# Attention and bilinear feed-forward on one core: the order of loads and of work in the opening list, the first weight block in halves, and eight weight columns in token halves

## The chip, the cores and the metric

The kernel runs on one core of a Trainium2 chip. The time is the device time of one execution in microseconds (us). The profile's span (first to last instruction) is about 1.8 us shorter than the time of the same run. Segments below are times in the span, and they come from profiled runs.

## The reference, cut to what matters

```python
# q, k, v: (8 batches, 8 heads, 576 tokens, 64);  bias_table: (32, 8)
scores = q @ k.T / 8 + bias_table[bucket(|i - j|)]      # per batch and head
attn   = softmax(scores) @ v
x      = attn.transpose(0, 2, 1, 3).reshape(4608, 512)
out    = ((x @ w_a) * (x @ w_b)) @ w_out                # 512 -> 1536 -> 512
```

The kernel works on pairs of heads: pair p is batch p // 4, heads 2(p % 4) and the next. The 576 tokens of a head are 512 in blocks of 128 and a tail of 64. The feed-forward part works in chunks of 512 tokens; a "weight column" is 128 of the 1536 columns of w_a or w_b.

## The kernel before

Pairs 8 to 31 run in a loop that is written as a pattern. What comes before, pairs 0 to 7 and the feed-forward inputs of chunk 0, is written as one list of tokens, in which each token is a few instructions. The order of the list is the order in which each engine gets its work.

```python
opening = """
    <k0 <q0 <k1 <q123h0 <k23 <tk <W0 <v0 <W1 <vtb <vta <tq <W2 <R0 <v1 <Wta <q123h1 <W3 <Wtb <R1
    <wa0 <k4 <wb0 <R2 <R3 <q4 <k5 <uq <q7 <q5 <wa1 <wb1 <k6 <uk <vt1b <k7 <vb1a <vb1b <vt1a <wa2 <q6
    <wb2 <wo TK0 PC0:A TQ0 PF1:D PX1:D PV1:A PU0:D CK0:A CQ00:D w1 S001 PX0:D CQ01:A S000 E001 E000
    # ... cut ...
    MT0 AV01 CX20:D M110 E111 N30 ET1 X30 M111 CQ31:A T2 ET2 S210 CX30:D E210 PF0:A LH FA0a N01 HA0a
    MT1 TK4 X01 T3 AV11 ET3 CX01:D S211 PU1:D FB0a FA1a E211 CK4:D HA1a N11 X11 G0a M210 S310 MT2
    # ... cut ...
    M73 M71 HA6f FB6f G6f AV50 N50 S62 ET6 MT6 E62 S61 FA7f HA7f M62 AV51 N51 TH S60 E61 M61 FB7f
    # ... cut ...
"""
for token in opening.split():
    step(token)
```

How to read a token:

| token | work | engine |
|---|---|---|
| `<q4 <k5 <v0 <vta <uq <wa0` | a load: queries, keys, values, tail values, tail queries of batch 1, a weight block | issued by GpSimd, in this order |
| `w1` | a filler matmul with zeros | TensorE |
| `TQ TK TZ`, `C...:A`, `C...:D` | transposes; the copy of their result, on ScalarE or VectorE | TensorE, then A or D |
| `S E M` | a block of scores, its exponential, its product with the band of bias values | TensorE, ScalarE, VectorE |
| `T ET MT`, `KS EK` | the same for the 64 tail tokens | the same three |
| `AV N X CX` | output of a pair, normalisation, its transposes, their copy | TensorE, VectorE, TensorE, A or D |
| `FA0a HA0a FB0a G0a` | weight column 0 of w_a for tokens 0 to 255, its eviction; the same of w_b; their product | TensorE, ScalarE, TensorE, VectorE |

`a` and `b` at the end of a weight column are the two token halves, `f` is all 512 tokens. The results of FA and FB go in turn to two PSUM banks, so a column has to wait until the one before the last is evicted.

```python
wrk   = ctx.enter_context(tc.tile_pool(name="wrk", bufs=2))
ps_ff = ctx.enter_context(tc.tile_pool(name="ps_ff", bufs=2, space=bass.MemoryType.PSUM))
XG = [wpool.tile([128, 5, 2, Dh], BF16, name=f"XG{i}") for i in range(2)]   # normalised output of pair p in XG[p % 2]

def ff_in(w, kind, c, df, lo, n):
    ps = ff_bank(f"{kind}{c}_{df}_{lo}")
    for mc in range(NMC):
        nc.tensor.matmul(out=ps[:, 0:n], lhsT=w[df // 4][:, mc, 128 * (df % 4):128 * (df % 4) + 128],
                         rhs=xn_sb[mc][:, 512 * c + lo:512 * c + lo + n],
                         start=(mc == 0), stop=(mc == NMC - 1))
    ff[kind, df, lo] = ps
```

The bias band (`<W`, `<R`, `<Wt`) is read from a table in memory that the kernel writes itself in its first microseconds, so the first band row in GpSimd's queue waits for that write.

The softmax here doesn't subtract the row's maximum and nothing guards it: scores larger than these inputs give would overflow.

## Time and profile before

| | before |
|---|---|
| time, median of 3 runs | 414.04 us (413.32 to 414.21) |
| span of the profiled run | 412.2 us |
| first weight column (FA0a) starts | 26.55 us |
| first score of pair 8, the end of the opening | 73.33 us |
| steady loop and end | 338.82 us |

The diff is in the opening alone, so the table cuts the span there. FA0a cuts the opening again. Ahead of it TensorE waits for ScalarE, VectorE and loads; after it TensorE is the bound. The page has one line on TensorE's granted clock, in tenths, in 40 slices of about 10.3 us:

```profile
PEclk9999999999999999999999999999999999999999
```

A 9 stands for 90% or more. The line says nothing about the time before the trace's first clock record, which here starts at 13.86 us; fillers of 0.61 us instead of 0.39 show half clock until then.

### The profile page before, as it was taken

The page shows a single profiled execution, that of the slowest core. Times are in us where ns is not written, and L with a number is a line of the kernel's source. Part 1 is how long each engine was busy: PE and PEld are TensorE (multiplying, and loading weights), DVE is VectorE, ACT ScalarE, POOL GpSimd, SP SyncE. Part 2 cuts the span into 40 slices and gives each one's busy share as a digit, 9 for nine tenths or more (in the row PEclk, how much of TensorE's full clock was granted, in tenths as well). Part 3 has the DMA queues.
Part 4 walks back from the last instruction along what each step waited for, and adds up shares of the span by engine and source line. Part 5 has one row for each costly group of instructions (what it writes and reads, how often), then busy time and mean ns, then how long its engine had stood idle before and what let it go on. Part 6 is the DMA issues. An engine that isn't in the chain of part 4 may idle for free.

```text
span 412.2 us, 8768 instructions
## 1 busy us (share of the span) xinstructions
PE 404.5 (98%) x3473; PEld 210.0 (51%) x3473; DVE 240.8 (58%) x568; ACT 251.3 (61%) x384; POOL 133.6 (32%) x191
## 2 busy tenths in 40 slices
PE   8999999999999999999999999999999999999996
PEld 3576656455555455455444555555545554444443
DVE  3898997366745665476656764667547652421320
ACT  4998992676748665677556765767486642322321
POOL 6967547788029300960079004300000000000000
PEclk9999999999999999999999999999999999999999
DMA  8999999999979914995299709960520012002004
GB/s 104 179 202 189 206 166 144 160 193 142 87 133 159 139 34 91 155 129 90 41 161 143 116 16 126 127 92 17 117 67 16 17 40 78 0 9 95 2 2 102
DMA packets 135786, 42.05 MB, mean 102 GB/s; under 512 B 113688, under 2 KB 130968, under 8 KB 135744
## 3 DMA queue, kind: packets, MB, share of 16 engines
q0 software_dynamic: 81712, 20.27, 56.3%
q1 hardware_dynamic: 48592, 11.87, 18.6%
q10 hardware_dynamic: 5440, 9.34, 7.2%
q8 instruction: 27, 0.44, 0.5%
q14 instruction: 15, 0.12, 0.1%
HBM read 39.18 MB, written 9.45 MB: 118 GB/s over the span
## 4 chain that ended last, share of the span: by engine, by line
PE 94%; DVE 2%; ACT 2%; DMA 1%; issue 1%; ACTq 0%; POOL 0%; POOLq 0%
PE pb L633 23%; PE pa L633 23%; PE po L670 22%; PE av L569 8%; PE qk L406 7%; PE av L559 2%; PE av L563 2%; PE qkh L446 1%; PE qkt L479 1%; DMA qn<-in_q_dram 1%; PE trb L321 1%; ACT ath L452 1%; PE trb L415 1%; PE trb L609 0%; DVE ath L461 0%
## 5 line engine op out<-in xcount | busy, mean ns | idle before, releaser
L430 ACT ACTIVATE at<-qk 128x1024 bf16<-128x1024 f32 x112 | 113.3, 1028 | 27.5 <-DMA out_dram<-ob 10.3
L643 DVE TENSOR_TENSOR g<-pb,ha 128x512 bf16<-128x512 f32 (+1 forms) x114 | 75.6, 664 | 75.0 <-PE pb L633 58.9
L633 PE MATMUL pb<-xn,wb 128*128 128x512 bf16 (+1 forms) x456 | 112.1, 368 | 0.2 <-DVE g L643 0.2
L633 PE MATMUL pa<-xn,wa 128*128 128x512 bf16 (+1 forms) x456 | 112.1, 368 | 0.0
L640 ACT ACTIVATE ha<-pa 128x512 f32<-128x512 f32 (+1 forms) x114 | 66.2, 581 | 67.7 <-PE pa L633 66.2
L670 PE MATMUL po<-wo,g 128*128 128x512 bf16 x420 | 98.2, 379 | 0.0
L435 DVE TENSOR_TENSOR at<-at,W 128x1024 bf16<-128x1024 bf16 x112 | 75.1, 686 | 22.2 <-ACT at L430 22.1
L633 PEld LDWEIGHTS <-wa 128*128 128x128 bf16 x456 | 41.2, 98 | 46.3 <-issue 6.6
L633 PEld LDWEIGHTS <-wb 128*128 128x128 bf16 x456 | 40.6, 97 | 43.6 <-issue 5.2
L670 PEld LDWEIGHTS <-g 128*128 128x128 bf16 x420 | 38.9, 98 | 44.9 <-issue 2.5
L675 ACT ACTIVATE ob<-po 128x512 f32<-128x512 f32 x34 | 20.4, 600 | 39.9 <-PE po L670 33.6
L569 PE MATMUL av<-vm,at 128*128 128x65 bf16 x896 | 41.2, 193 | 0.0
L569 PEld LDWEIGHTS <-at 128*128 128x128 bf16 x896 | 37.4, 97 | 6.3
L132 POOL DMA_DIRECT2D qn<-in_q_dram x48 | 36.4, 807 | 12.0 <-PE qk L406 6.9
L170 POOL DMA_DIRECT2D vt<-in_v_dram x12 | 7.4, 620 | 98.9 <-PE av L563 98.1
L580 DVE RECIPROCAL rc<-av 128x6 f32<-128x6 f32 (+1 forms) x64 | 11.9, 186 | 45.2 <-PE av L569 40.8
L141 POOL DMA_DIRECT2D kn<-in_k_dram x48 | 36.2, 794 | 1.4 <-issue 0.7
L559 PE MATMUL av<-vt,att 128*128 128x130 bf16 x152 | 33.6, 221 | 0.0
L406 PE MATMUL qk<-QB,KB 64*128 64x512 bf16 x192 | 29.1, 381 | 0.0
L582 DVE TENSOR_TENSOR XG<-av,rc 128x384 bf16<-128x384 f32 (+2 forms) x64 | 27.2, 425 | 2.2
L506 ACT ACTIVATE att<-qkt 128x640 bf16<-128x640 f32 x24 | 16.8, 701 | 13.0 <-PE qkt L480 13.0
L559 PEld LDWEIGHTS <-att 128*128 128x128 bf16 x152 | 15.0, 98 | 6.5
(104 smaller groups left out, 327.0 us busy)
## 6 DMA issues: line engine op xcount, KB each, us to landing
out_dram<-ob ACTq DMA_DIRECT2D x31, 256.0 KB, 3.1
vn<-in_v_dram POOLq DMA_DIRECT2D x16, 256.0 KB, 5.8
kn<-in_k_dram POOLq DMA_DIRECT2D x48, 64.0 KB, 5.0
qn<-in_q_dram POOLq DMA_DIRECT2D x48, 64.0 KB, 4.4
wa<-in_moe_w_a_dram POOLq DMA_DIRECT2D x3, 512.0 KB, 7.4
wb<-in_moe_w_b_dram POOLq DMA_DIRECT2D x3, 512.0 KB, 9.2
wo<-in_moe_w_out_dram POOLq DMA_DIRECT2D x1, 1536.0 KB, 15.6
xn<-XG SPq DMA_TRANSPOSE x52, 3.0
```

The lines of the kernel that those rows point to most:

```text
L132: nc.gpsimd.dma_start(out=by_tile(qn[b % 2])[:, h0 // 4, t, :, :], in_=q[b, h0:h1, 128 * t:128 * t + 128, :].transpose([1, 0, 2]))
L141: nc.gpsimd.dma_start(out=by_tile(kn[b % 2])[:, h0 // 4, t, :, :], in_=k[b, h0:h1, t:SM:NM, :].transpose([1, 0, 2]))
L406: nc.tensor.matmul(out=ps[:, hh, :], lhsT=kT[r, t, :], rhs=qT[r, :, :], start=True, stop=True)
L430: nc.scalar.activation(out=at[:, :, :], in_=ps[:, :, :], func=ACTF.Exp, scale=scale)
L435: nc.vector.tensor_tensor(out=at[:, :, :], in0=at[:, :, :], in1=w[:, :, S - 1 + t:S - 1 + t - SM:-1], op=MULT)
L559: nc.tensor.matmul(out=pav[:, slot, :, :], lhsT=weights_tail(p, jq), rhs=vt[i][:, :, hp, :], start=True, stop=True)
L569: nc.tensor.matmul(out=pav[:, slot, hh, :], lhsT=weights(p, t, hh, jq), rhs=vm[i][:, 2 * hp + hh, t, :], start=False, stop=True, skip_grou ...
L582: nc.vector.tensor_tensor(out=xg[:, jqs[0]:jqs[0] + m, :, :], in0=pav[:, 0:m, :, 0:Dh], in1=rc[:, 0:m, :].unsqueeze(3).to_broadcast([128, ...
L633: nc.tensor.matmul(out=ps[:, 0:n], lhsT=w[df // 4][:, mc, 128 * (df % 4):128 * (df % 4) + 128], rhs=xn_sb[mc][:, 512 * c + lo:512 * c + lo ...
L640: nc.scalar.activation(out=ha[:, 0:n], in_=ff["pa", df, lo][:, 0:n], func=ACTF.Copy)
L643: nc.vector.tensor_tensor(out=g_sb[df][:, lo:lo + n], in0=ff["pb", df, lo][:, 0:n], in1=ff["ha", df, lo][:, 0:n], op=MULT)
L670: nc.tensor.matmul(out=po[:, :], lhsT=g_sb[df][:, 128 * tt:128 * tt + 128], rhs=wo_sb[:, df, :], start=(df == 0), stop=(df == NDF - 1))
```

## The change

It has three parts. Loads: queries go first, and half of the values of batch 0 (four of its eight heads) and half of its tail values go ahead of the first band row, so that they no longer wait for the bias table. Weights: the first block of w_a and of w_b is stored and loaded in two halves, so that the first columns of both are there sooner. Work: eight weight columns instead of six are done in token halves, and the whole list after the loads is put in another order.

```diff
-    wa_sb = [wpool.tile([128, NMC, WC], BF16, name=f"wa{i}") for i in range(NW)]
+    wa_sb = [wpool.tile([128, 1 + (i == 0), NMC, WC // (1 + (i == 0))], BF16, name=f"wa{i}")
+             for i in range(NW)]
@@ (wb_sb the same) ... cut ... @@
-    def load_weights(src, dst, part):
+    def load_weights(src, dst, part, half):
+        c0 = WC * part + WC // 2 * half
+        n = WC // (1 + (part == 0))
         nc.gpsimd.dma_start(
-            out=dst[part][:, :, :],
-            in_=src[:, WC * part:WC * part + WC].rearrange("(m p) n -> p m n", p=128))
+            out=dst[part][:, half, :, :],
+            in_=src[:, c0:c0 + n].rearrange("(m p) n -> p m n", p=128))
@@ ... cut ... @@
-            parts = [(range(0, 6), 0, 256), (range(0, 6), 256, 256), (range(6, NDF), 0, 512)]
+            parts = [(range(0, 8), 0, 256), (range(0, 8), 256, 256), (range(8, NDF), 0, 512)]
@@ opening, ... cut ... @@
-        <k0 <q0 <k1 <q123h0 <k23 <tk <W0 <v0 <W1 <vtb <vta <tq <W2 <R0 <v1 <Wta <q123h1 <W3 <Wtb <R1
-        <wa0 <k4 <wb0 <R2 <R3 <q4 <k5 <uq <q7 <q5 <wa1 <wb1 <k6 <uk <vt1b <k7 <vb1a <vb1b <vt1a <wa2 <q6
-        <wb2 <wo TK0 PC0:A TQ0 PF1:D PX1:D PV1:A PU0:D CK0:A CQ00:D w1 S001 PX0:D CQ01:A S000 E001 E000
+        <q0 <k0 <q123h0 <tk <k23 <k1 <vta <v0 <W2 <W0 <tq <vtb <W1 <v1 <W3 <R0 <q123h1 <Wtb <Wta <R1 <k4
+        <q5 <wa0a <wb0a <k5 <uq <R2 <R3 <wa0b <wb0b <q4 <vt1b <wa1 <k7 <wb1 <k6 <q7 <vt1a <wb2 <uk <vb1b
+        <vb1a <wa2 <q6 <wo PU0:A w1 TQ0 PX1:A PC0:A PF0:D TK0 PC1:A CK0:D CQ00:A CQ01:A w1 S000 PV1:D
@@ ... cut ... @@
+        N01 M111 ET2 FA0a FB0a HA0a E210 T3 TZ0x CZ0x:A G0a FA1a HA1a MT2 AV11 ET3 M210 N11 S211 E211
+        FB1a G1a X01 TK5 CK5:D FA2a HA2a CX01:D S310 S311 E310 M211 FB2a FA3a G2a MT3 TQ4 E311 M311 TQ5
@@ ... cut ... @@
```

More of the change, by code (lines that the diff above doesn't have):

```diff
@@ L108 @@
     WC = DF // NW
-    wa_sb = [wpool.tile([128, NMC, WC], BF16, name=f"wa{i}") for i in range(NW)]
-    wb_sb = [wpool.tile([128, NMC, WC], BF16, name=f"wb{i}") for i in range(NW)]
+    wa_sb = [wpool.tile([128, 1 + (i == 0), NMC, WC // (1 + (i == 0))], BF16, name=f"wa{i}")
+             for i in range(NW)]
+    wb_sb = [wpool.tile([128, 1 + (i == 0), NMC, WC // (1 + (i == 0))], BF16, name=f"wb{i}")
+             for i in range(NW)]
     wo_sb = wpool.tile([128, NDF, DM], BF16, name="wo")
@@ L297, in load @@
         else:
-            load_weights(*((moe_w_a, wa_sb) if name[1] == "a" else (moe_w_b, wb_sb)), int(name[2]))
+            load_weights(*((moe_w_a, wa_sb) if name[1] == "a" else (moe_w_b, wb_sb)), int(name[2]), int(name[-1] == "b"))
     st = [dict() for _ in range(NP)]
@@ L628, in ff_bank, with block @@
         return ps_ff.tile([128, 512], FP32, tag="ffn", name=name)
+    def block(w, df, mc):
+        half, d = divmod(df % 4, 2) if df < 4 else (0, df % 4)
+        return w[df // 4][:, half, mc, 128 * d:128 * d + 128]
     def ff_in(w, kind, c, df, lo, n):
@@ L632, in ff_in @@
         for mc in range(NMC):
-            nc.tensor.matmul(out=ps[:, 0:n], lhsT=w[df // 4][:, mc, 128 * (df % 4):128 * (df % 4) + 128],
+            nc.tensor.matmul(out=ps[:, 0:n], lhsT=block(w, df, mc),
                              rhs=xn_sb[mc][:, 512 * c + lo:512 * c + lo + n],
@@ L728 @@
     opening = """
-        <k0 <q0 <k1 <q123h0 <k23 <tk <W0 <v0 <W1 <vtb <vta <tq <W2 <R0 <v1 <Wta <q123h1 <W3 <Wtb <R1
-        <wa0 <k4 <wb0 <R2 <R3 <q4 <k5 <uq <q7 <q5 <wa1 <wb1 <k6 <uk <vt1b <k7 <vb1a <vb1b <vt1a <wa2 <q6
-        <wb2 <wo TK0 PC0:A TQ0 PF1:D PX1:D PV1:A PU0:D CK0:A CQ00:D w1 S001 PX0:D CQ01:A S000 E001 E000
-        w1 TQ30 PC1:D TK1 CK1:D TQ10 CQ10:D S011 E011 CQ30:D TK3 S100 E100 TZ1 CK3:D S301 M001 TQ20
-        PV0:D TK2 E301 S101 E101 CQ20:D CK2:D w1 S200 E200 CZ1:D M000 w1 KS w1 S201 EK w2 S010 E201 V0:D
@@ L734 @@
-        M101 TZ0 M100 M200 M201 AV00 N00 CZ0:A AV10 E010 X00 CX00:A S300 E300 N10 T0 V1:D X10 CX10:A
-        M010 ET0 AV20 TQ11 TQ21 M011 N20 CQ11:A S110 S111 CQ21:A E110 X20 M301 TQ31 M300 AV30 T1 PW:D
-        MT0 AV01 CX20:D M110 E111 N30 ET1 X30 M111 CQ31:A T2 ET2 S210 CX30:D E210 PF0:A LH FA0a N01 HA0a
-        MT1 TK4 X01 T3 AV11 ET3 CX01:D S211 PU1:D FB0a FA1a E211 CK4:D HA1a N11 X11 G0a M210 S310 MT2
-        CX11:A E310 FB1a G1a S311 FA2a HA2a TQ4 M211 CQ4:A FB2a AV21 E311 FA3a HA3a TQ5 MT3 M310 S43 S42
@@ L739 @@
-        CQ5:A G2a FB3a N21 M311 TK5 E43 E42 TZ0x G3a CZ0x:D AV31 LV CK5:D N31 FA4a HA4a X21 TQ7 CQ7:A
-        S41 E41 S52 E52 CX21:D FB4a FA5a HA5a X31 G4a TK6 M43 FB5a CX31:D S40 E40 S53 G5a FA0b FB0b
-        CK6:D M41 TZ1x HA0b G0b CZ1x:D S51 FA1b FB1b E53 M53 HA1b G1b E51 TK7 CK7:D M40 FA2b HA2b S50
-        E50 FB2b FA3b G2b HA3b V2:D T4 FB3b FA4b V3:D ET4 G3b S70 E70 M42 MT4 M52 HA4b FB4b G4b TQ6 T5
-        ET5 M50 CQ6:A AV40 N40 MT5 M51 FA5b S71 E71 HA5b S73 FB5b AV41 G5b M70 N41 S72 E73 FA6f E72 T6
@@ L744 @@
-        M73 M71 HA6f FB6f G6f AV50 N50 S62 ET6 MT6 E62 S61 FA7f HA7f M62 AV51 N51 TH S60 E61 M61 FB7f
-        G7f E60 M60 S63 E63 M63 FA8f HA8f M72 T7 FB8f G8f AV60 N60 ET7 MT7 FA9f HA9f FB9f G9f AV70 FA10f
-        FB10f N70 HA10f G10f AV71 FA11f N71 FB11f X71 HA11f G11f AV61 N61 X70 FO00 FO01 FO02 HO0 CX70:D
-        CX71:D
+        <q0 <k0 <q123h0 <tk <k23 <k1 <vta <v0 <W2 <W0 <tq <vtb <W1 <v1 <W3 <R0 <q123h1 <Wtb <Wta <R1 <k4
+        <q5 <wa0a <wb0a <k5 <uq <R2 <R3 <wa0b <wb0b <q4 <vt1b <wa1 <k7 <wb1 <k6 <q7 <vt1a <wb2 <uk <vb1b
@@ new lines @@
+        <vb1a <wa2 <q6 <wo PU0:A w1 TQ0 PX1:A PC0:A PF0:D TK0 PC1:A CK0:D CQ00:A CQ01:A w1 S000 PV1:D
+        PF1:D PU1:D E000 TQ10 TQ30 CQ30:D S001 CQ10:D S010 TQ20 TK2 E001 PX0:D S011 E010 PV0:D E011
+        CQ20:D TZ1 CK2:D S200 E200 CZ1:D TK1 TK3 S201 E201 CK1:D CK3:D V0:D w1 S101 E101 M200 w2 S100
+        E100 w2 KS EK S300 E300 M201 M001 TZ0 CZ0:A M000 M100 M101 V1:D AV00 N00 AV10 N10 S301 X00 M300
+        E301 T0 X10 AV20 CX00:A CX10:D M301 TQ11 TQ31 ET0 AV30 CQ11:A S111 M011 N20 CQ31:A S110 TQ21 LH
@@ new lines @@
+        E111 TK4 E110 M010 PW:D MT0 N30 CQ21:A CK4:D T1 AV01 X30 M110 X20 CX20:D T2 ET1 MT1 S210 CX30:A
+        N01 M111 ET2 FA0a FB0a HA0a E210 T3 TZ0x CZ0x:A G0a FA1a HA1a MT2 AV11 ET3 M210 N11 S211 E211
+        FB1a G1a X01 TK5 CK5:D FA2a HA2a CX01:D S310 S311 E310 M211 FB2a FA3a G2a MT3 TQ4 E311 M311 TQ5
+        M310 FB3a AV21 N21 HA3a CQ4:A S40 G3a CQ5:A S43 E40 FA4a E43 X11 HA4a M40 AV31 LV S53 CX11:D E53
+        S52 E52 FB4a N31 FA5a G4a M53 HA5a X31 X21 FB5a CX21:D CX31:D G5a S41 S51 E41 FA6a HA6a TK6 E51
@@ new lines @@
+        TK7 S42 FB6a FA7a E42 M41 CK7:D CK6:D TZ1x G6a HA7a TQ7 CQ7:A S50 FB7a M43 FA0b CZ1x:D G7a E50
+        M51 HA0b V2:D T4 ET4 FB0b G0b S70 M42 FA1b FB1b HA1b MT4 T5 E70 G1b FA2b HA2b ET5 AV40 M50 N40
+        FB2b FA3b HA3b S71 E71 S72 G2b FB3b FA4b HA4b MT5 AV41 G3b M52 N41 E72 S73 E73 FB4b FA5b G4b
+        HA5b AV50 N50 FB5b FA6b G5b TQ6 HA6b AV51 FB6b FA7b CQ6:A HA7b M71 M70 G6b T7 ET7 FB7b FA8f N51
+        TH HA8f M72 S60 E60 G7b S61 FB8f E61 MT7 FA9f V3:D M73 AV70 G8f HA9f S63 E63 S62 E62 FB9f M60
@@ L748 @@
+        N70 FA10f M61 HA10f T6 ET6 G9f M62 AV71 M63 N71 FB10f FA11f MT6 HA11f G10f X71 CX71:A AV60 N60
+        FB11f G11f FO00 AV61 X70 CX70:A FO01 FO02 N61 HO0
     """
```

## The prediction

> **What bounds the kernel now.** I read the page first, then the engines' busy time in five stretches, then the timeline of TensorE and of GpSimd over the first 75 us, then the chain of waits over the first 54 us, and last the start times of single matmuls.
>
> ```profile
> PE 404.5 (98%) x3473; PEld 210.0 (51%) x3473; DVE 240.8 (58%) x568; ACT 251.3 (61%) x384; POOL 133.6 (32%) x191
> ...
> core 0: us, PE busy (x) PEld busy (x) DVE busy (x) ACT busy (x) POOL busy (x), PEclk, DMA share, GB/s
> 0.00:13.86 13.86, 11.81 (x102) 5.30 (x102) 6.94 (x27) 8.10 (x11) 10.15 (x19) 1.00 0.94 118
> 13.86:23.54 9.68, 8.26 (x131) 5.35 (x129) 9.04 (x22) 9.21 (x14) 9.68 (x15) 1.00 1.12 182
> 23.54:53.00 29.46, 29.44 (x404) 20.61 (x404) 27.03 (x79) 27.01 (x44) 16.52 (x23) 1.00 1.34 203
> 53.00:73.30 20.30, 20.30 (x208) 11.65 (x206) 16.52 (x45) 10.69 (x16) 13.52 (x20) 1.00 1.77 153
> 73.30:412.20 338.90, 334.65 (x2634) 167.06 (x2633) 181.31 (x400) 196.31 (x301) 83.75 (x118) 1.00 0.71 87
> ```
>
> The reader is to see two regimes. From 23.5 us on TensorE has no idle time worth the name. The last 338.9 us are the steady loop, which the diff does not touch. The change therefore acts on the first 73.3 us alone (the opening list ends there, at the first score matmul of pair 8), and there it can gain in two ways only: less waiting before 23.5 us, or fewer nanoseconds per matmul after it. In 13.86 to 23.54 ScalarE (9.21 of 9.68) and VectorE (9.04) are the full engines, and TensorE waits for them.
>
> I then summed each matmul's start-to-start time and took off its streaming time (109 ns for 256 columns, 216 for 512, 59 for 130, 33 for 65, 28 for a 64-wide pair). Left over: 7.8 us before 13.88 us, 3.7 us in 13.88 to 23.53, 0.4 us to 26.5, and 4.8 us in 26.5 to 73.3. The last number is not idle time; it is this:
>
> ```profile
> 29.44 0.61 PE L633 MATMUL pb<-xn,wb 128*128 128x256 bf16 x4
> 29.89 0.60 PE L633 MATMUL pa<-xn,wa 128*128 128x256 bf16 x4
> ...
> 30.60 0.39 PE L446 MATMUL qkh<-QT,KT 64*128 64x256 bf16 x4
> 30.93 0.61 PE L633 MATMUL pb<-xn,wb 128*128 128x256 bf16 x4
> 31.47 0.39 PE L446 MATMUL qkh<-QT,KT 64*128 64x256 bf16 x4
> ```
>
> Columns are start and duration. Four 256-column matmuls take 0.45 us when more weight columns follow (29.44 to 29.89) and 0.54 when 64-row scores follow (30.93 to 31.47). The scores take 0.33 (30.60 to 30.93) where two pairs should stream in 0.22. So each **switch of array shape** (64-row scores, 64-wide transposes, full array) costs about 0.1 us. In the opening list I count 44 switches from the first weight column (FA0a) on: 4.83 / 44 = 0.110 us each.
>
> Before 13.9 us the array is slow:
>
> ```profile
> 8.33 0.61 PE L237 MATMUL warm<-zero_sb 128*128 128x512 bf16 x1
> ...
> 13.88 0.39 PE L237 MATMUL warm<-zero_sb 128*128 128x512 bf16 x1
> ```
>
> The same filler takes 0.61 and then 0.39; the trace's full-clock record starts at 13.863 us. The chain and GpSimd's timeline give the rest:
>
> ```profile
> 2.06 4.09 DMA qn<-in_q_dram
> 13.99 1.94 ACT ath L452 x2
> 17.80 0.70 DVE ath L461
> ...
> 4.91 0.74 POOL L158 DMA_DIRECT2D tlc<-in_k_dram  x1
> 8.31 0.72 POOL L252 DMA_DIRECT2D W<-bias_tab  x1 [2.66 <-DMA bias_tab<-wo]
> 9.02 0.78 POOL L123 DMA_DIRECT2D vn<-in_v_dram  x1
> ```
>
> The first query lands at 6.16. GpSimd, which issues all loads in order at some 0.72 us each, then stands 2.66 us until the bias table is in memory; values of batch 0 are queued behind that wait though they do not need it.
>
> **What the Trainium skill says.** (1) "TensorE: Matmul & The Clock Gate", Part 1: the array starts at half clock and is released after a busy window of about 3.4 us. The trace agrees on two clocks (0.61 against 0.39), but release came only at 13.86, four such windows in, so early density matters. (2) Same page, "Back-to-back issue gap": N/2.4 + 2.5 ns. The trace has 109 and 216 ns, so splitting a 512-column matmul costs 2 x 109 - 216 = 2 ns. (3) "DMA: Bandwidth & Descriptors", "Measured": 1 MB moves at 341 GB/s, smaller transfers less efficiently. Here the first 1 MB (f32) block of wa landed 4.03 us after its predecessor (25.33 against 21.30), 260 GB/s; a half is then about 2 us, perhaps a little more. (4) "Perfetto Trace Analysis", "Identifying the Most-Contended Engine": matmul busy share is a poor measure. The trace agrees: 100% busy hides the 4.8 us above.
>
> **The change, part by part.**
>
> *Order of work after FA0a.* The new list has 35 switches there, not 44 (65 against 75 in the whole opening): scores and transposes stand together more often. 9 x 0.110 = **-0.98 us**. TensorE is the bound there, so this goes straight to the end, if the order brings no new wait.
>
> *Two more columns in halves.* 2 columns x 2 matrices x 4 blocks x 2 ns = +0.03 us on TensorE. ScalarE: an eviction starts its successor after 0.264 us (256) or 0.494 (512), so +0.03 each. VectorE: 2 x 0.341 - 0.608 = +0.07 each. Some 0.2 us, beside TensorE's work. **+0.03**.
>
> *Values ahead of band rows.* One half-batch of values (0.78 us of issue) and one half of the tail values (0.65) move into the 2.66 us wait. All behind them is issued 0.78 + 0.65 = 1.4 us earlier. It is not on the path by itself: no matmul after 6.2 us is shown waiting for a load. It makes the new order possible. **0**.
>
> *Halved weights.* The new list puts FB0a right after FA0a, where the old one had 2.9 us between them. Whole, the first wb landed at 28.68; 1.4 us earlier is 27.3, too late for a start at about 26.4. Halved and behind two more loads (0.7 us each), I put the two first halves at about 23.2 and 24.9. **0**, an enabler, with two more issues of some 0.8 us on a GpSimd that waits anyhow.
>
> *The first 24 us*, walked by hand with the durations of the trace (exp 1.02, next starts after 0.92; band multiply 0.60; normalisation 0.18 + 0.42; transposes 0.57 and a four-matmul score 0.54 at half clock, 0.34 and 0.33 at full). q first lands at 4.4, k at 6.2; scores S000 at 7.3, exp at 7.9 (now 8.0). Pair 0's four score blocks need no further load, so ScalarE runs to 12.0 with one gap of 0.3; TensorE waits for the keys of pairs 2 and 3 at about 10.0. Two gaps of 0.6 follow (score buffers). Before the last scores of pair 1 (S111) ScalarE has done 12 blocks in both lists: 22.31 before, about 22.0 in the new. By AV01 I get 24.4 against 24.5, with the keys of pair 4 transposed already (0.34): together 0.44. **-0.4**.
>
> *Added risk.* FB4a comes at about 37.4, and its weights land at about 37.3: +0.2. Pair 5's output (N51) now has some 13.7 us of TensorE work left before pair 8, instead of 14.9; the transposed queries landed at 72.14, 1.2 us before use: +0.1. Together **+0.3**. The sum is -0.98 + 0.03 - 0.4 + 0.3 = -1.05. Some weight on a later clock (third rival, 0.3 x 1.0) is set off by the chance of an earlier one. 414.04 - 1.05 = 413.0; as a list retuned as a whole is more likely to have been kept for a gain than my walk can see, I go 0.2 lower: **412.8 us**.
>
> **Rivals.** *One: a new wait takes the place.* Weights or queries arrive late for the tighter order (FB4a, or the queries of pair 4 now queued behind four weight halves). For: margins of 0 to 2 us by my walk. Against: ScalarE and VectorE have 2.4 us each free in 23.5 to 53. It would give 413.5 to 415. *Two: everything is hidden.* The ScalarE and VectorE sequence up to 23.5 sets the start of the saturated stretch, and switches are traded for small stalls: 413.8 to 414.2. Against: the 0.1 us per switch is there at each of them. *Three: the clock.* Fillers move: before S000 the new list has two instead of one, but only one more until V0, where the old had five by then, and TensorE waits about 0.6 us for keys. If release slips by one window of 3.4 us, some 2.4 us of work takes 4.8 instead of fitting 3.4: +1 to +1.5, so 413.8 to 414.5. If it comes a window early, 411.5 to 412. *Four: the denser exp stream gains more than I walked*, up to the 3.7 us of leftover in 13.88 to 23.53; half of it gives 411.
>
> **Range and chances.** The mean effect is -1.2 with about 1.5 us of spread from clock, walk and landings: 410.8 to 414.8. For 2% (8.3 us) on the fast side the opening would have to lose more than all of the leftover after 13.88 us; on the slow side it needs a wait of 8 us. Faster 0.015, same 0.965, slower 0.02.
>
> **What would show it.** Right: TensorE's sums of leftover time after 26 us fall by about 1 us; the first matmul of the steady loop starts near 72.1 instead of 73.33; the steady loop keeps its 338.9 us; GpSimd's wait for the bias table shrinks to about 1.2 us and the first half of wa lands before 24; exps up to 22 us have gaps below 2 us in sum. Wrong: waits of TensorE on DMA at weight columns or at queries of batch 1 or 2, fillers of 0.61 us after 14 us, or a longer steady loop.

## The result, and the profile after

The changed kernel took 413.09 us (median of 4 runs, 412.45 to 414.06), the kernel before 413.96 (median of 4, 413.32 to 414.21). The ratio is 0.9983, with a 95% interval of 0.996 to 1.0006. Six more runs in the experiments below gave 412.72 and 0.9961 (0.9938 to 0.9984). The first interval includes 1, the second does not. The change is small, in the direction and of the size that was predicted. Where it comes from is another matter, and the traces tell it differently from the prediction.

These are the busy line and the clock line of the page of the kernel after:

```profile
PE 399.6 (97%) x3439; PEld 211.5 (51%) x3489; DVE 239.7 (58%) x566; ACT 253.0 (61%) x390; POOL 135.3 (33%) x193
...
PEclk9799999999999999999999999999999999999999
```

The 5 us by which PE fell are not a gain: this trace has 50 matmul records fewer than weight loads (3439 against 3489), and some matmuls of the steady loop are simply missing from it. So the times below are start times. The 7 in the clock line is new: in the second slice the clock was low. The five stretches of the prediction's table, for the kernel after (the last cut at the new end of the opening):

```profile
core 0: us, PE busy (x) PEld busy (x) DVE busy (x) ACT busy (x) POOL busy (x), PEclk, DMA share, GB/s
0.00:13.86 13.86, 10.45 (x102) 4.76 (x103) 7.61 (x29) 8.76 (x14) 11.91 (x21) 0.81 1.04 131
13.86:23.54 9.68, 8.61 (x146) 5.82 (x148) 8.60 (x19) 8.42 (x13) 9.68 (x14) 0.92 1.20 187
23.54:53.00 29.46, 28.77 (x386) 21.12 (x386) 26.06 (x79) 27.40 (x45) 16.29 (x23) 1.00 1.35 204
53.00:72.98 19.98, 19.82 (x225) 12.73 (x226) 16.14 (x43) 11.80 (x21) 13.01 (x19) 1.00 1.78 140
72.98:411.50 338.52, 331.90 (x2589) 167.09 (x2633) 181.32 (x400) 196.59 (x301) 84.43 (x119) 1.00 0.69 88
```

The columns are the stretch, its length, each engine's busy time with its count, then the granted clock. The clock is 0.81 and 0.92 in the first two stretches. The opening ends at 72.98 instead of 73.33, and the rest takes 338.5 instead of 338.8. Cut at the same three places, the two profiled runs differ like this:

| stretch | before | after | difference |
|---|---|---|---|
| start to FA0a | 26.55 | 26.89 | +0.34 |
| FA0a to first score of pair 8 | 46.78 | 46.09 | -0.69 |
| steady loop and end | 338.82 | 338.51 | -0.31 |
| span | 412.16 | 411.48 | -0.67 |

**The work after FA0a.** TensorE's timeline of the kernel after; columns are start, duration, engine, line, operation, tiles, shapes and count:

```profile
26.89 0.61 PE L641 MATMUL pa<-xn,wa 128*128 128x256 bf16 x4
27.34 0.60 PE L641 MATMUL pb<-xn,wb 128*128 128x256 bf16 x4
...
31.98 0.61 PE L450 MATMUL qkh<-QT,KT 64*128 64x256 bf16 x8
32.52 0.61 PE L641 MATMUL pb<-xn,wb 128*128 128x256 bf16 x4
32.97 0.60 PE L641 MATMUL pa<-xn,wa 128*128 128x256 bf16 x4
33.50 0.64 PE L325 MATMUL trb<-ident,qn 128*64 128x128 bf16 x16
```

FB0a now follows FA0a after 0.45 us; before, 2.89 us lay between them. Scores and transposes stand in groups of eight and sixteen where the old list had four and eight. Eight scores take 0.54 us (31.98 to 32.52); twice four took 2 x 0.33. Not all of the 0.69 us that this stretch lost is a gain: by the streaming times of its matmuls, 0.19 us of it is work that the new list does ahead of FA0a (the four matmuls whose records are missing here are counted in). The other 0.50 us are less time lost between matmuls.

**The loads.** GpSimd's timeline of the kernel after:

```profile
5.60 0.69 POOL L267 DMA_DIRECT2D vt<-in_v_dram  x1
6.22 0.81 POOL L125 DMA_DIRECT2D vn<-in_v_dram  x1
7.94 1.42 POOL L254 DMA_DIRECT2D W<-bias_tab  x2 [0.91 <-DMA bias_tab<-wo]
```

The two loads of values stand where GpSimd used to wait, and its wait is down from 2.66 to 0.91 us. The first halves of wa and wb landed at 24.04 and 25.42 us; the whole blocks had landed at 25.33 and 28.68.

**The first 15 us.** TensorE's timeline of the kernel after again:

```profile
6.75 0.41 PE L325 MATMUL trk<-ident,kn 128*64 128x128 bf16 x8 [1.17 <-DMA kn<-in_k_dram]
...
9.22 0.61 PE L450 MATMUL qkh<-QT,KT 64*128 64x256 bf16 x4 [0.43 <-ACT ath L456]
...
14.47 1.03 PE L239 MATMUL warm<-zero_sb 128*128 128x512 bf16 x2
15.44 0.40 PE L450 MATMUL qkh<-QT,KT 64*128 64x256 bf16 x4
```

The clock record of this run is full from 5.25 to 8.66, half until 15.49, and full from there. The same four scores take 0.61 us inside the half-clock stretch and 0.40 after it. In its first window at full clock TensorE waited 1.17 us for the first keys; they landed at 6.70.

**The steady loop.** It holds the same instructions in the same order in both kernels, and yet it differs by 0.31 us. The two traces run at a constant distance until one multiply on VectorE. First VectorE's timeline before, then after:

```profile
221.18 0.69 DVE L643 TENSOR_TENSOR g<-pb,ha 128x512 bf16<-128x512 f32 x1 [0.94 <-ACT att L422]
```

```profile
220.47 0.69 DVE L651 TENSOR_TENSOR g<-pb,ha 128x512 bf16<-128x512 f32 x1 [0.59 <-PE pb L641]
```

The bracket is the wait and what ended it. After, the multiply is released by its own matmul. Before, it is released by a later exponential of ScalarE, although its input from ScalarE (ha) was done more than a microsecond earlier; that costs 0.35 us, and a matmul behind it waits 0.17. All 14 profiles fall in two groups here. The three kernels with six columns in halves (before, values_first, before_clock) have loops of 338.81 to 338.87, and values_first and before_clock show the same release by the exponential. All eleven with eight columns in halves have 338.48 to 338.51. So the 0.3 us belongs to the part "eight columns", though it falls 150 us later. Why the number of columns alters what that multiply waits for was not found.

### The profile page after: what moved, and what is told of

It reads as the page before. It is cut to its first block, busy times and chain, and to the rows that moved or that the text cites. A ratio compares the mean times of both kernels' runs of the same rounds, so it can differ in the third digit from the quotient of the medians.

```text
span 411.5 us, 8761 instructions
## 1 busy us (share of the span) xinstructions
PE 399.6 (97%) x3439; PEld 211.5 (51%) x3489; DVE 239.7 (58%) x566; ACT 253.0 (61%) x390; POOL 135.3 (33%) x193
## 4 chain that ended last, share of the span: by engine, by line
PE 94%; ACT 2%; issue 1%; DMA 1%; DVE 1%; ACTq 0%; POOL 0%; POOLq 0%
PE pb L641 23%; PE pa L641 23%; PE po L678 22%; PE av L573 8%; PE qk L410 7%; PE av L563 2%; PE av L567 2%; PE qkt L483 1%; PE qkh L450 1%; DMA kn<-in_k_dram 1%; ACT ath L456 1%; PE trb L419 1%; PE trb L325 1%; PE trk L325 0%; PE trb L613 0%
## 5 line engine op out<-in xcount | busy, mean ns | idle before, releaser
L434 ACT ACTIVATE at<-qk 128x1024 bf16<-128x1024 f32 x112 | 113.5, 1031 | 27.8 <-DMA out_dram<-ob 10.3
L678 PE MATMUL po<-wo,g 128*128 128x512 bf16 x403 | 95.7, 379 | 0.8
L439 DVE TENSOR_TENSOR at<-at,W 128x1024 bf16<-128x1024 bf16 x112 | 75.2, 686 | 22.5 <-ACT at L434 22.4
L641 PEld LDWEIGHTS <-wa 128*128 128x128 bf16 x464 | 42.5, 98 | 46.1 <-issue 5.7
L586 DVE TENSOR_TENSOR XG<-av,rc 128x384 bf16<-128x384 f32 (+1 forms) x64 | 27.2, 424 | 2.2
```

Source lines behind the costliest of these rows:

```text
L434: nc.scalar.activation(out=at[:, :, :], in_=ps[:, :, :], func=ACTF.Exp, scale=scale)
L439: nc.vector.tensor_tensor(out=at[:, :, :], in0=at[:, :, :], in1=w[:, :, S - 1 + t:S - 1 + t - SM:-1], op=MULT)
L586: nc.vector.tensor_tensor(out=xg[:, jqs[0]:jqs[0] + m, :, :], in0=pav[:, 0:m, :, 0:Dh], in1=rc[:, 0:m, :].unsqueeze(3).to_broadcast([128, ...
L641: nc.tensor.matmul(out=ps[:, 0:n], lhsT=block(w, df, mc), rhs=xn_sb[mc][:, 512 * c + lo:512 * c + lo + n], start=(mc == 0), stop=(mc == NM ...
L678: nc.tensor.matmul(out=po[:, :], lhsT=g_sb[df][:, 128 * tt:128 * tt + 128], rhs=wo_sb[:, df, :], start=(df == 0), stop=(df == NDF - 1))
```

## The experiments

Eleven new kernels ran, and the changed one once more, in four calls, each on another chip. "Timed" is the median of six runs (lowest to highest), with the ratio to the kernel before of the same rounds. The last three columns are from the one profiled run of each.

| label | built on | timed, us | ratio (95%) | FA0a | pair 8 | FA0a to pair 8 |
|---|---|---|---|---|---|---|
| (before) | | 413.96 (4 runs) | | 26.55 | 73.33 | 46.78 |
| (after) | | 413.09 (4 runs) | 0.9983 (0.996-1.0006) | 26.89 | 72.98 | 46.09 |
| after_again | after | 412.72 (411.10-413.73) | 0.9961 (0.9938-0.9984) | 26.89 | 72.89 | 46.00 |
| keep_clock | after | 412.79 (411.75-414.31) | 0.9969 (0.9947-0.9991) | 25.50 | 72.88 | 47.37 |
| whole_weights | after | 415.96 (413.35-417.76) | 1.0045 (1.0015-1.0075) | 25.32 | 75.85 | 50.53 |
| more_switches | after | 413.69 (413.09-414.67) | 0.999 (0.9973-1.0007) | 26.35 | 73.41 | 47.06 |
| values_first | before | 414.58 (414.19-415.50) | 1.0017 (0.9994-1.0041) | 27.15 | 73.93 | 46.78 |
| eight_columns | before | 414.69 (414.44-415.46) | 1.0018 (0.9997-1.0039) | 26.53 | 74.42 | 47.88 |
| before_clock | before | 413.69 (412.71-414.72) | 0.9991 (0.9967-1.0015) | 25.34 | 72.12 | 46.78 |
| third_xg | keep_clock | 412.52 (411.72-413.06) | 0.9962 (0.9941-0.9984) | 25.63 | 72.58 | 46.95 |
| values_late | after | 413.58 (412.88-414.84) | 0.9997 (0.9977-1.0017) | 25.94 | 74.54 | 48.60 |
| eight_in_turn | before | 415.18 (413.87-416.05) | 1.0031 (1.0011-1.0052) | 25.13 | 73.59 | 48.46 |
| tails_early | third_xg | 412.23 (411.30-413.26) | 0.9964 (0.9946-0.9983) | 27.00 | 72.99 | 45.99 |
| fill_keys | tails_early | 412.40 (411.96-413.29) | 0.9964 (0.9949-0.9979) | 25.79 | 71.78 | 45.99 |

The runs of the kernel before in the four calls had medians of 414.10, 414.07, 413.78 and 414.30 (11 runs in each); the first four labels belong to the first call, the next four to the second, then three to the third, and fill_keys to the fourth. All outputs were correct.

### The same kernel again: after_again

No edit. It gives the scatter and the reference.

> The changed kernel once more, on the same chip as the three that follow, so that they can be compared with it. Both theories: 0.998 of the kernel before, 412.4 to 414.1. What it is for: in the first profile the array was at full clock from 5.25 to 8.66 us, at half clock to 15.49, and full after that. If the phase of the clock varies from run to run, the record will lie elsewhere here, and the first score matmul of pair 8 (72.98 in the first profile) moves with it by some tenths of a microsecond.

It measured 412.72, a ratio of 0.9961. The two sets of runs of the changed kernel give ratios of 0.9983 and 0.9961; what is common to them is a gain of about 0.2 to 0.4%. The profiled segments repeat to 0.1 us. The runs scatter over 2.6 us, so a difference of half a microsecond between two medians of six is not a finding.

The clock record of this profile lies where the first one did: full from 5.08 to 8.50 us, half until 15.32. The six runs don't all share it. Each run's result lists the mean clock that was granted over the span, and one window of 3.41 us at half clock takes 0.004 off this mean. Three of the six have 0.992 to 0.994 and took 412.13, 413.20 and 413.32 us; three have 0.999 or 1.000 and took 411.10, 412.24 and 413.73. So the clock varies from run to run, but it doesn't sort these times.

### Is it the switches: more_switches

The old spacing is put back at six places. Nothing else is touched, and there are 46 switches after FA0a in place of 35.

```diff
-S310 S311 E310 M211 FB2a
+S310 E310 M211 FB2a S311
-S40 G3a CQ5:A S43 E40 FA4a E43
+S40 G3a CQ5:A E40 FA4a S43 E43
-S53 CX11:D E53 S52 E52 FB4a
+S53 CX11:D E53 FB4a S52 E52
-G5a S41 S51 E41 FA6a HA6a
+G5a S41 E41 FA6a S51 HA6a
-G7b S61 FB8f E61
+G7b FB8f S61 E61
-S63 E63 S62 E62 FB9f
+S63 E63 FB9f S62 E62
```

> The changed kernel with score blocks that stand together put apart by weight columns, in six places: 46 switches of array shape from FA0a on, not 35. Theory (0.105 us a switch, TensorE the bound there): 11 x 0.105 = 1.15 us, the steady loop starts 0.9 to 1.3 us later than in after_again, 414.0 to 414.5 in all. Rival (switches are hidden behind ScalarE and VectorE): less than 0.3 us.

The timeline of TensorE in more_switches, at one of the six places:

```profile
35.21 0.39 PE L410 MATMUL qk<-QT,KT 64*128 64x512 bf16 x2
35.53 0.61 PE L641 MATMUL pa<-xn,wa 128*128 128x256 bf16 x4
36.07 0.39 PE L410 MATMUL qk<-QT,KT 64*128 64x512 bf16 x2
36.40 0.34 PE L613 MATMUL trb<-ident,XG 128*128 128x128 bf16 x3
```

Two scores, four weight matmuls and two scores take 1.19 us (35.21 to 36.40). In the changed kernel four scores and four weight matmuls take 0.98 (from 35.54 to 36.52). FA0a to pair 8 takes 47.06 instead of 46.00 to 46.09, so 11 switches cost 0.97 to 1.06 us, about 0.09 each. The times agree, 413.69 against 412.72, but the two intervals of the ratios overlap, so the times alone would not show it. Pair 8 came only 0.52 us later than in after_again, and not 0.9 to 1.3 as expected, because FA0a, which lies ahead of the edit, came 0.54 us earlier in this run. In the stretch that was edited this part does what the prediction said of it, and nearly at its size.

### Is it the halved weights: whole_weights

The changed kernel with the first blocks whole again, in the place of their first halves.

```diff
-<wa0a <wb0a <k5 <uq <R2 <R3 <wa0b <wb0b
+<wa0 <wb0 <k5 <uq <R2 <R3
-    wa_sb = [wpool.tile([128, 1 + (i == 0), NMC, WC // (1 + (i == 0))], BF16, name=f"wa{i}")
+    wa_sb = [wpool.tile([128, 1, NMC, WC], BF16, name=f"wa{i}")
```

> The changed kernel with whole weight blocks in the place of the first halves. Theory (halving is what lets FB0a stand right after FA0a): wa lands at about 25.2 and wb at about 27.9, so TensorE waits some 0.5 to 0.9 us for wb at FB0a, and the steady loop starts 0.4 to 0.9 us later than in after_again. Rival (the block would have been there in time, or ScalarE and VectorE catch up): no later by more than 0.15 us.

TensorE's timeline of whole_weights:

```profile
28.92 0.62 PE L641 MATMUL pb<-xn,wb 128*128 128x256 bf16 x4 [2.98 <-DMA wb<-in_moe_w_b_dram]
...
30.54 1.04 PE L641 MATMUL pa<-xn,wa 128*128 128x256 bf16 x4
...
33.34 0.61 PE L641 MATMUL pb<-xn,wb 128*128 128x256 bf16 x4
```

FB0a stands 2.98 us waiting for wb, and then the same four matmuls take 1.04 us until they are back at 0.61: the clock record is half from 29.4 to 32.8. The wait is paid, and then about 1.7 us on top (an estimate: half of the 3.4 us at half clock). In time it is 415.96 against 412.72, so +3.2 us, with intervals that do not overlap. Only 0.4 to 0.9 us were expected, but wb landed at 28.87 and not at 27.9, TensorE was there 1.57 us earlier than in the kernel after (FA0a at 25.32), and the loss of the clock was not foreseen. The halves earn nothing by themselves; without them the new order would be slower than the old one (ratio 1.0045).

### Are the loads the gain: values_first and values_late

values_first puts the values ahead of the band rows in the kernel before. values_late puts them behind the first band row in the kernel after.

```diff
 values_first, on the kernel before
-<tk <W0 <v0 <W1 <vtb <vta <tq
+<tk <vta <v0 <W0 <W1 <vtb <tq
 values_late, on the kernel after
-<k1 <vta <v0 <W2 <W0 <tq
+<k1 <W2 <vta <v0 <W0 <tq
```

> The kernel before with one part of the change alone: values and half of the tail values of batch 0 issued ahead of the band rows on GpSimd's queue. Theory (no matmul of the kernel before waits for those loads, so the part only makes the new order possible): GpSimd's 2.66 us wait for the bias table shrinks to about 1.2 us, everything behind lands some 1.4 us earlier, and the steady loop still starts at 73.2 to 73.5; time within 0.15% of the kernel before. Rival (the earlier loads are the gain of the change): 0.3 to 1 us earlier.

> The changed kernel with the values back behind the first band row on GpSimd's queue, as in the kernel before; the rest of the change kept. Theory (in the new order loads land just in time, so the earlier issue is an enabler like the halves): everything behind lands 1 to 1.4 us later, the query tails of batch 1 (landed at 26 to 28, read at 28.4) and the key tails (42.6, read at 43.0) are waited for, and the steady loop starts 0.5 to 1.2 us later than in after_again, if the clock's record is alike. Rival (the place of the values is indifferent here as it was in values_first): within 0.3 us.

values_first: 414.58 against 414.07, a ratio of 1.0017. Nothing is gained, and FA0a to pair 8 takes the same 46.78. Pair 8 starts at 73.93 and not at 73.2 to 73.5, because this run was slower ahead of FA0a (its clock record is half from 11.02 to 17.84). values_late: 413.58 against 413.78; against the 412.72 of after_again, from another call, it is 0.9 us longer, or 1.2 if each is set against the kernel before of its own call; the intervals of the ratios overlap. Two waits on loads appear. The first line is from TensorE's timeline of values_late, the second from its table of waits (engine, tile, line, what it waited for, total us, times, longest):

```profile
28.25 0.29 PE L365 MATMUL trb<-ident,tlc 64*128 64x64 bf16 x4 [0.77 <-DMA tlc<-in_q_dram]
```

```profile
PE pb L641 <- DMA wb<-in_moe_w_b_dram: 0.9, 1, 0.9
```

The tail queries of batch 1 and the second block of wb arrive 0.8 and 0.9 us late. Pair 8 starts 1.65 us later than in after_again, where 0.5 to 1.2 were expected. This profiled run held the full clock from 4.97 us on, so keep_clock below is closer to it: there FA0a to pair 8 takes 47.37, here 48.60. The move of the values is an enabler as well: it is worth nothing in the old order and about a microsecond in the new one, where everything behind it in the queue is needed on time.

### Two more columns in halves: eight_columns and eight_in_turn

The kernel before with columns 6 and 7 in halves, first with the halves of one matrix side by side, then with FA and FB in turn and other work between them.

```diff
 eight_columns, on the kernel before (and parts with 8)
-FA6f E72 T6 M73 M71 HA6f FB6f G6f
+FA6a FA6b E72 T6 M73 M71 HA6a HA6b FB6a FB6b G6a G6b
-FA7f HA7f M62 AV51 N51 TH S60 E61 M61 FB7f G7f
+FA7a FA7b HA7a HA7b M62 AV51 N51 TH S60 E61 M61 FB7a FB7b G7a G7b
 eight_in_turn, on eight_columns
-FA6a FA6b E72 T6 M73 M71 HA6a HA6b FB6a FB6b G6a G6b AV50 N50
+FA6a E72 T6 M73 M71 HA6a FB6a G6a FA6b HA6b AV50 FB6b G6b N50
-FA7a FA7b HA7a HA7b M62 AV51 N51 TH S60 E61 M61 FB7a FB7b G7a G7b
+FA7a HA7a M62 AV51 FB7a N51 G7a TH S60 E61 FA7b HA7b M61 FB7b G7b
```

> The kernel before with eight weight columns of chunk 0 in halves instead of six, order otherwise unchanged. Theory: two halves of 109 ns for one of 216 cost TensorE nothing, ScalarE and VectorE 0.2 us beside it; steady loop starts 0 to 0.2 us later. Rival (the small instructions crowd ScalarE and VectorE in a stretch where they are 90% busy): 0.3 us later or more.

> The kernel before with eight columns in halves once more, but each half evicted before the next two are begun, so that two wa halves never hold both banks. Theory (the 0.86 us of waits in eight_columns came from my placing of the evictions, not from the halves): from the first weight column to pair 8 46.8 to 47.0 us, as in the kernel before (46.78), not 47.88. Rival (halves cost in this stretch however they are placed): 47.3 or more.

TensorE's timeline of eight_columns:

```profile
54.68 1.03 PE L633 MATMUL pb<-xn,wb 128*128 128x256 bf16 x8 [0.34 <-ACT ha L640]
...
60.94 1.02 PE L633 MATMUL pa<-xn,wa 128*128 128x512 bf16 x4 [0.52 <-DVE g L643]
```

FA0a to pair 8 is 1.10 us longer, and 0.86 of it are these two waits for evictions. Two halves take 0.45 us each on TensorE and fill both banks; the next column then waits for ScalarE or VectorE. In turn it is no better: 415.18, and FA0a to pair 8 takes 48.46. TensorE's timeline of eight_in_turn has two waits for weights, which came up only because TensorE reached them earlier in that run:

```profile
25.13 0.61 PE L633 MATMUL pa<-xn,wa 128*128 128x256 bf16 x4 [0.67 <-DMA wa<-in_moe_w_a_dram]
...
28.34 0.61 PE L633 MATMUL pb<-xn,wb 128*128 128x256 bf16 x4 [0.24 <-DMA wb<-in_moe_w_b_dram]
```

The first wait ends where FA0a starts, so it lies ahead of the segment; only the second is in it. That leaves 48.22, which is 1.4 us over the old list, and 1.3 of them are four gaps of 0.24 to 0.45 us between TensorE's start times from 52 to 60 us, where the halved columns are. So both runs came out as the rivals of their expectations say: halves cost in this stretch. In time the part by itself costs 0.6 us (eight_columns, whose interval includes no difference) to 1.4 us (eight_in_turn, clear of noise), in spite of the 0.3 us that it gains in the steady loop. Another placing in the old order might do better; none was tried. The changed kernel has it spread over columns 0 to 7, in its new order.

### The clock: keep_clock and before_clock

Fillers where TensorE waits in the first 10 us, in the kernel after and in the kernel before.

```diff
 keep_clock, on the kernel after
-w1 TQ0 PX1:A
+w1 TQ0 w4 PX1:A
-S001 CQ10:D S010
+S001 w2 CQ10:D S010
 before_clock, on the kernel before
-TK0 PC0:A TQ0
+TK0 w3 PC0:A TQ0
```

> The changed kernel with four more fillers where TensorE waits 1.2 us for the first keys, and two where it waits 0.4 us for a score buffer. Clock theory (the 1.2 us of idleness costs the full clock that had just been granted, and 8.66 to 15.49 us then run at half): the half-clock stretch vanishes or ends a window earlier, and the steady loop starts 0.3 to 0.8 us earlier, at 72.2 to 72.7; 412.3 to 412.8 in all. Rival (ScalarE and VectorE set the pace up to 24 us anyway): start between 72.8 and 73.2 whatever the clock does. If the fillers themselves cost: up to +0.4.

> The kernel before with three fillers in TensorE's 0.9 us wait for the first query, to hold the clock there too. If the clock is what the change lost in its first stretch and not something of the new order: full clock from about 5 us on here as well, first weight column (26.55 in the kernel before) up to 1 us earlier, steady loop 0.4 to 1 us earlier. If VectorE and ScalarE set the pace: first weight column within 0.3 us of 26.55.

Both profiled runs have full clock from about 5 us until within 0.1 us of the end of the span. FA0a starts at 25.50 in keep_clock, 1.39 us earlier than in the kernel after, and at 25.34 in before_clock, 1.21 earlier than before. So a late clock cost the profiled run of each kernel over a microsecond ahead of FA0a. At equal clock the new list is not ahead there: 25.50 against 25.34, with 0.22 us more work of TensorE in it, worked out from the streaming times. In keep_clock the gain is then lost to the last tenth, since pair 8 starts at 72.88, as in after_again. TensorE's and VectorE's timelines of keep_clock show to what:

```profile
25.50 0.61 PE L641 MATMUL pa<-xn,wa 128*128 128x256 bf16 x4
...
27.71 0.29 PE L365 MATMUL trb<-ident,tlc 64*128 64x64 bf16 x4 [0.67 <-DMA tlc<-in_q_dram]
```

```profile
63.37 0.56 DVE L586 TENSOR_TENSOR XG<-av,rc 128x384 bf16<-128x384 f32 x1 [1.32 <-DMA xn<-XG]
```

The tail queries cost 0.83 us between matmuls there, of which the line shows 0.67. VectorE then stands 1.32 us because pair 7's normalised output goes to the buffer out of which pair 5's transposing transfer still reads; TensorE loses 0.57 of that. In time keep_clock (412.79) equals the changed kernel (412.72), and before_clock (413.69, ratio 0.9991) is within the interval of the kernel before. The profiled run of before_clock was the fastest of its six, at 412.71; the others took 412.9 to 414.7. By the number, keep_clock came out as its rival said (72.88, in 72.8 to 73.2), but not for the rival's reason, since FA0a did come 1.39 us earlier. before_clock came out as the clock theory said and a little beyond it: FA0a and pair 8 both 1.21 us earlier.

The mean clocks of the timed runs tell whether the fillers held the clock there too. All six runs of keep_clock, and all of third_xg and fill_keys below, have 0.998 or more, so none of these 18 lost a window of full clock in the opening once it was granted. (The 0.998 comes from half clock at the very end: values_late has it with a record that is full from 4.97 to 411.15.) Of the ten runs of the changed kernel seven have 0.992 to 0.995. So the fillers hold the clock in the timed runs as in the profiled one, and the times still do not follow it: the runs of keep_clock took 411.75 to 414.31. For kernels without fillers the mean says less, since the profiled run of the kernel before has 1.000 with a record that starts only at 13.86. Of the 44 runs of the kernel before, 20 have 0.998 or more and 24 less, and both groups have a median of 414.04.

### Taking those waits away: third_xg, tails_early, fill_keys

Each of these removes the wait that the one before it showed. third_xg gives pair 5 a buffer of its own and loads the tail queries one place earlier. tails_early loads the tail keys and the values of batch 1 ahead of the last block of wb. fill_keys has fillers where tails_early lost its clock.

```diff
 third_xg, on keep_clock
-<wb0a <k5 <uq <R2
+<wb0a <uq <k5 <R2
-XG = [... for i in range(2)]
+XG = [... for i in range(3)]      # pair 5 uses XG[2]
 tails_early, on third_xg
-<vt1a <wb2 <uk <vb1b <vb1a <wa2
+<vt1a <uk <vb1a <vb1b <wb2 <wa2
 fill_keys, on tails_early
-S010 TQ20 TK2 E001
+S010 TQ20 w3 TK2 E001
```

> The kernel of keep_clock with the two waits taken away that ate its 1.39 us: the query tails of batch 1 (uq) issued one load earlier, and the output of pair 5 in a buffer of its own, so that pair 7's normalisation need not wait for pair 5's transposing DMA. Theory (after the clock is held, landings of loads and of that DMA end the waits, 0.83 and 0.57 us): steady loop starts at 71.6 to 72.1 instead of 72.88, 411.5 to 412.1 in all. Rival (the next wait stands right behind, at the transposed queries of batch 2, which landed at about 71.6): 71.9 to 72.8.

> The kernel of third_xg with the key tails of batch 1 and its values ahead of the last wb block on GpSimd's queue, against the 0.83 us that TensorE waited for those tails. Theory (the landings set the end of each wait): that wait goes and the steady loop starts at 71.6 to 72.0, 411.2 to 411.9 in all, the fastest of all. Rival (once more the next load stands right behind): 72.2 or later.

> The kernel of tails_early with three more fillers before the keys of pairs 2 and 3, where its profiled run waited 1.6 us and lost the full clock at 11.5 us. Theory (idle TensorE in the first 14 us loses the clock, and a held clock with the tails in time is worth the whole 1.4 us): the clock record has one stretch only, the first weight column comes at 25.3 to 25.8, the steady loop starts at 71.5 to 72.1, and the median is 411.3 to 412.0. Rival (what the opening gains, some later landing takes): steady loop at 72.4 or later, median 412.2 or more, as for keep_clock and third_xg.

In third_xg both waits are gone, and another load is the next limit: pair 8 starts at 72.58, in the rival's range. TensorE's timeline:

```profile
42.63 0.29 PE L366 MATMUL trb<-ident,tlc 64*128 64x64 bf16 x4 [0.83 <-DMA tlc<-in_k_dram]
```

In tails_early that is gone too and FA0a to pair 8 takes 45.99, but in this run TensorE waited for the keys of pairs 2 and 3 (landed 10.94) and lost the clock:

```profile
10.99 0.41 PE L326 MATMUL trk<-ident,kn 128*64 128x128 bf16 x8 [1.59 <-DMA kn<-in_k_dram]
```

Pair 8 starts at 72.99, not at 71.6 to 72.0. But this profiled run is not typical: it is the slowest of the six (413.26; the others took 411.30 to 412.45) and the only one with a mean clock under 0.998 (0.995). The wait that fill_keys fills cost the clock in one run of six.

fill_keys has full clock from 5.4 us on and no wait on a load after its start. This is the longest line of TensorE's table of waits, after that of the first filler:

```profile
PE qkh L451 <- ACT ath L457: 0.5, 2, 0.3
```

And this is the first score of pair 8, from its timeline:

```profile
71.78 0.61 PE L411 MATMUL qk<-QB,KB 64*128 64x512 bf16 x4
```

What is left are waits for ScalarE of at most 0.5 us. Pair 8 starts at 71.78: the shortest opening of all profiles, 1.2 us below the changed kernel's. In time it is 412.40, a ratio of 0.9964 (0.9949 to 0.9979). tails_early has 412.23 and 0.9964, the changed kernel 0.9961 and 0.9983. No version was shown to beat the changed kernel. So fill_keys starts pair 8 when the theory says, and has the median that the rival says (412.2 or more). Against tails_early its fillers had little to win, as five of six runs there held the clock already. Why the 1.2 us against the changed kernel do not appear in the median was not settled; a lost clock is not the reason, since all six runs of fill_keys have 0.998 or more, and one profiled run of each kernel, with scatter of 1 to 3 us between runs, can't decide it.

### How busy is busy enough

The clock changes in these records come at multiples of about 3.41 us. These are rows of the table by stretch, each one such window at full clock, of three kernels, after, tails_early and before_clock (same columns as above):

```profile
5.25:8.66 3.41, 2.02 (x41) 1.16 (x42) 1.30 (x5) 1.18 (x3) 2.50 (x5) 1.00 1.34 152
```

```profile
8.10:11.50 3.40, 1.65 (x29) 0.84 (x27) 1.62 (x6) 2.40 (x3) 3.07 (x5) 1.00 1.38 211
```

```profile
8.30:11.70 3.40, 2.65 (x58) 1.75 (x58) 2.15 (x5) 2.55 (x3) 3.40 (x6) 1.00 1.17 154
```

After the first two windows, with 59% and 49% busy (2.02 / 3.41 and 1.65 / 3.40), the clock was halved. After the third, with 78%, it stayed. In whole_weights the window before the loss had 14% (0.48 of 3.40). Two more rows, of values_first and of eight_columns, keep this from being a rule:

```profile
4.19:7.60 3.41, 1.89 (x27) 1.02 (x25) 1.49 (x7) 1.00 (x3) 2.83 (x4) 1.00 1.19 153
```

```profile
7.56:10.97 3.41, 2.52 (x47) 1.45 (x45) 1.52 (x5) 2.83 (x4) 3.41 (x6) 1.00 1.31 160
```

After the first, with 55%, the clock stayed; after the second, with 74%, it was halved. So the busy share of a window does not tell by itself what follows, and no limit was found. Busy times of TensorE are modelled, so the shares are rough; but it did not take a window without work to lose the clock.

## Why the prediction was right or wrong

The total was right: 412.8 predicted, 413.09 and 412.72 measured. It was partly right by compensation, and the steps have to be judged one by one.

**Switches, -0.98: the mechanism is shown, the size was somewhat too large.** The count mixes two ways. The 44 switches of the old list include the one into pair 8, the 35 of the new one do not; counted alike, in the traces and in the lists, they are 44 and 36, so 8 fewer and not 9. Summed over the changes of shape alone, the time lost is 4.7 us at 44 before and 3.8 us at 36 after, 0.107 each, so the switches gave about 0.87. more_switches puts 11 switches back and loses 1.0 us in the segment and in the time, 0.09 each net of other waits where the prediction had 0.110. This is the bulk of what the change gains.

**"Added risk", +0.3: the term that was mis-sized.** The leftover after FA0a (time less streaming time, as the prediction has it) fell from 4.82 to 4.32, so by 0.5 and not by 0.98. The 36 changes of shape at 0.107 make 3.85 of the new leftover; the other half microsecond are small waits, most of them new (the same sum leaves 0.1 of the old leftover), such as 0.11 at 27.8 and 0.25 at 45.3. The two places that the prediction named for its risk did not cost anything in the kernel after: FB4a started at 38.29, and its weights had landed at 38.01.

**Two more columns in halves, +0.03: wrong.** The working counted the engines' extra time and left out the two banks. Done alone in the old list this part costs 1.10 us in the segment, 0.86 of it in waits for evictions, and 0.6 us in time, which is within the noise. In the steady loop it gave 0.31 us back, which nothing in the prediction foresaw: it said that the loop keeps its 338.9 us, and the loop took 338.5.

**Values first, 0, and halved weights, 0: right, as enablers.** values_first gains nothing in the old list. In the new list their removal costs 3.2 us (whole_weights), clear of noise, and about 1 us (values_late), shown by two waits in the profile but not clear of noise in time. The first halves landed at 24.04 and 25.42, predicted at 23.2 and 24.9, and GpSimd's wait fell to 0.91, predicted about 1.2.

**The first 24 us, -0.4: wrong.** The profiled run reached FA0a 0.34 us later, not 0.4 earlier. The step that failed is the walk's start: keys were put at 6.2 and landed at 6.70, the first scores at 7.3 and started at 7.71. Behind it stands the third rival, "the clock", which happened in another form. The prediction expected a release that slips. The release came early, at 5.25, and was lost again at 8.66 for two windows. The Trainium skill, "TensorE: Matmul & The Clock Gate", Part 1, says that the array falls back after an idle window of about 3.4 us; here the longest wait in the window before the loss was 1.17 us. The prediction's own sign for "wrong", fillers at half clock after 14 us, is in the trace at 14.47. At equal clock (keep_clock and before_clock) the walk's 0.4 is not there either: the new list is 0.16 us later at FA0a with 0.22 us more work in it, so about even.

**The rivals.** The first, a new wait, holds in part for the kernel after (the half microsecond) and fully for its variants: whenever TensorE came earlier, a load or a buffer was the next limit (tail queries, pair 5's transfer, tail keys). The second, all hidden, falls with more_switches. The third is above. The fourth, a denser stream of exponentials, is not in the traces: ahead of 22.5 us ScalarE has 12 exponentials in both profiled runs.

**Signs.** The steady loop was to start near 72.1; it started at 72.98 and 72.89. So the opening gave 0.4 us, not 1.2. The leftover after FA0a fell by 0.5 us where about 1 was named, and the first half of wa landed at 24.04, not before 24. The rest of the measured gain is the loop's 0.3 and, in after_again, scatter that the profiles do not resolve.

Open are three things: why the clock's first release and loss vary from run to run, why the number of halved columns changes one wait 150 us later, and why the shorter openings of keep_clock and its successors do not show in the medians, although their runs held the clock.

## What to carry to other kernels

Where TensorE is the bound, count how often the list changes the array's shape and group what has the same shape; then try that count alone, as more_switches does, before believing it. Loads moved earlier and blocks cut smaller earn nothing by themselves, but a denser order stands on them, and each gain uncovers the next load that is only just in time. Compare openings of two kernels only after looking at the clock record of both runs, since a wait of a microsecond in the first ten was followed here by two windows of half clock. And look at the mean clock of every timed run before building on one profiled run, which can be the odd one out, as it was for tails_early.

## What the Trainium skill lacked or had wrong

- "TensorE: Matmul & The Clock Gate", "Back-to-back issue gap": the page calls the formula the gap of an isolated matmul and says that it over-counts in a stream at 512 columns, about 216 ns where 131 were measured. Here the streams of one shape, with a weight load for each matmul, follow the formula: 109 and 216 ns for 256 and 512 columns.
- No page was found to give what a change of array shape costs. ("TensorEngine Tiling (Array Packing)", "Key Properties", says that a change of tiling mode drains TensorE, without a figure.) Eleven such changes cost 0.97 to 1.06 us here, about 0.09 us each.
- "TensorE: Matmul & The Clock Gate", Part 1, states release after one busy window of about 3.4 us and a fall back after an idle one. The records here change at multiples of 3.41 us, which agrees. The fall back came also after windows that were 59% and 49% busy, with no wait over 1.6 us in them, and once after one of 74% (eight_columns), while the clock stayed after one of 55% (values_first). It lasted one window (tails_early, whole_weights) or two (after). Release came at 13.86 us in the kernel before, after a window with TensorE busy throughout (7.03 to 10.45) that had not released it.
- "DMA: Bandwidth & Descriptors", "Measured": its sizes have nothing between 64 KB and 1 MB. With other loads in flight, a 0.5 MB half of the weights landed 1.38 us behind the half before it (24.04 and 25.42), and in whole_weights a 1 MB block 3.59 us behind the other (25.28 and 28.87). A plan for loads that must arrive just in time can't be made from the table alone.
- "Perfetto Trace Analysis", "Matmuls", says to rotate matmul groups through PSUM banks, so that evictions overlap the next group. No page was found on what it costs when two banks turn and a group is shorter than its eviction. Two more columns in halves, which the streaming formula puts at 0.03 us, lengthened the segment by 1.10 us, of which 0.86 were waits for ScalarE and VectorE.
